# Head-pair loads in one DMA each, bucket bits carried by small DMAs, and the weight split on GpSimd, in a fused kernel of hashed attention and a gated Fourier convolution

## The chip, the core and the metric

The kernel runs on one core of one Trainium2 chip. A core has five engines with a program of their own each: TensorE (PE in the profile, with its weight loads as PEld), VectorE (DVE), ScalarE (ACT), GpSimd (POOL) and SyncE (SP), which here only issues DMAs. Each engine works through its own instructions in order. The metric is device microseconds of one execution; lower is better. Ratios are computed as the mean time of one kernel's fast runs over the mean time of the other's fast runs of the same rounds on the same chip, so they are not quite the ratio of the medians that are quoted beside them.

## The reference

Two stages follow each other. The first is attention in 4 batches of 8 heads with 768 tokens and head size 64, in which a query sees only the keys of its own bucket; the bucket is the sign pattern of six projections.

```python
q_bits = (np.einsum('bhsd,dk->bhsk', q, proj) > 0)         # 6 bits a token
k_bits = (np.einsum('bhsd,dk->bhsk', k, proj) > 0)
mask = q_bucket[:, :, :, None] == k_bucket[:, :, None, :]  # the six bits read as a number
scores = np.where(mask, scale * q @ k.T, -1e9)
attn = softmax(scores); out = attn @ v                     # the divisor gets + 1e-9
# ... heads side by side: x is (4, 768, 512) ...
x1, x2, x3 = split(x @ w_proj)                             # w_proj is (512, 1536)
x2_conv = irfft(rfft(x2, axis=1) * rfft(filter, axis=0))   # over the 768 tokens
y = x1 * x2_conv * x3
return y @ w_out                                           # (4, 768, 512)
```

## The kernel before

The kernel works on 16 head pairs. For each pair a preparation loads q and k, transposes them on TensorE, evacuates them to `tz`, multiplies with the projection (`zps`, the "bit matmuls"), and turns the signs into six rows of ±0.5, which are appended to q and k, so that one matmul yields score and bucket match together. Preparations run two pairs ahead. GpSimd copies `tz` to fp16 rows. Then come scores (`stp`), exponentials (`pt`, ScalarE), the product with v (`pv`), its evacuation (`S` on ScalarE, `T` on VectorE), and the divisors (`lt`, `rl`, `rdr`, `R`, by way of DMAs on SyncE). Weights and filter are loaded and split into two fp16 halves while the first pairs run.

```python
def nat_load(src, b, pr, which, eng):          # q, k: 4 DMAs each; v: 2
    shape = [P, 2, 3, 2, HD] if which == "v" else [P, 3, 2, 2, HD]
    t_ = natp.tile(shape, FP32, tag="nat", name=f"nat_{which}")
    for par in range(2):
        head = src[b, 2 * pr + par].rearrange("(c p j) d -> p c j d", c=3, p=P, j=2)
        if which == "v":
            eng.dma_start(t_[:, par], head)
        else:
            for j in range(2):
                eng.dma_start(t_[:, :, j, par, :], head[:, :, j, :])
    return t_
# ... prep_gen: the transposes, each half evacuated to tz on VectorE, rows copied on GpSimd ...
        with tc.high_priority(offset=200):     # the bit matmuls of both halves, at once
            for hf in range(2):
                cs = slice(HALF * hf, HALF * hf + HALF)
                zps = psW.tile([P, HALF], FP32, tag="w", name="zps")
                zs.append(zps)
                for i in (1, 0):
                    mm = nc.tensor.matmul(zps[64 * i : 64 * i + 38, :], projpad, tzs[i][:, cs])
                    # ...
        for hf in range(2):                    # eight evacuations of 6 rows
            for i, which in enumerate(("q", "k")):
                for par, r0 in ((0, 64), (1, 0)):
                    z0 = 64 * i + 32 * par
                    nc.vector.tensor_scalar(row[(which, par)][r0 : r0 + 6, cs],
                        zs[hf][z0 : z0 + 6, :], 0.0, 0.5, ALU.is_gt, ALU.subtract)
        yield 1700
# ... setup_gen, for each of four 128x1536 chunks of w_proj:
            nc.vector.tensor_copy(th, w32)
            (nc.vector if c % 2 else nc.gpsimd).tensor_tensor(tl, w32, th, ALU.subtract)
```

A generator's `yield n` ends a turn of n nanoseconds of TensorE's time; a loop deals such turns out to attention, preparation and the second stage, and so fixes the order of TensorE's program. PSUM tiles with tag "w" share four banks: `tps`, `zps`, `pv` and all of the second stage's.

The softmax here doesn't subtract the row's maximum and nothing guards it: scores larger than these inputs give would overflow.

## Time and profile before

The kernel before took 524.32 us (median of 3 runs, 521.95 to 526.36). The first lines of its profile page give the span and each engine's busy time, its share of the span, and its instructions.

```profile
span 521.2 us, 7013 instructions
## 1 busy us (share of the span) xinstructions
PE 469.4 (90%) x2552; PEld 248.6 (48%) x2552; DVE 322.5 (62%) x591; ACT 229.8 (44%) x321; POOL 156.1 (30%) x206
```

TensorE is busy nine tenths of the time. Where it is not shows the view by stretches: for each stretch of time, its length, then each engine's busy us and number of instructions, TensorE's granted clock, DMA share and rate.

```profile
core 0: us, PE busy (x) PEld busy (x) DVE busy (x) ACT busy (x) POOL busy (x), PEclk, DMA share, GB/s
...
58.00:92.00 34.00, 23.04 (x98) 10.51 (x98) 28.31 (x38) 9.93 (x14) 23.98 (x21) 0.80 0.42 114
...
120.00:270.00 150.00, 140.05 (x771) 75.48 (x770) 89.58 (x173) 72.36 (x100) 44.30 (x59) 0.98 0.26 65
270.00:425.00 155.00, 147.17 (x838) 80.44 (x836) 98.22 (x189) 78.75 (x111) 37.97 (x47) 1.00 0.19 51
...
```

Between 58 and 92 us TensorE worked 23 of 34 us at a clock of 0.80. Between 120 and 425 us it missed 18 of 305 us. The number of matmuls in parentheses will be the measure of progress below: every kernel here has 2552 of them, so whoever has issued more by a given time is ahead. The measure is rough by a few: a matmul across the border of two stretches is counted in both (counted by their starts, the leads below differ by up to 4), and matmuls are not all of one length.

A wait of ScalarE of 13.3 us and two of TensorE's waits on `tz` are in the view of waits (the engine and line that waited, whom for, us in total, times, the longest).

```profile
ACT S L275 <- DVE T L276: 13.3, 1, 13.3
...
PE zps L215 <- DVE tz L202: 5.6, 4, 2.5
...
PE tps_k L198 <- DVE tz L202: 2.2, 1, 2.2
```

VectorE was what ScalarE waited 13.3 us for. The timeline (start, duration, engine, line, operation, tiles) shows why it was late: two equal casts, and a subtraction of GpSimd.

```profile
52.13 0.41 DVE L435 CAST woh_622<-o_616 128x512 f16<-128x512 f32 x1
...
53.33 3.31 DVE L435 CAST woh_626<-o_616 128x512 f16<-128x512 f32 x1
...
56.32 3.93 POOL L438 TENSOR_TENSOR wol_620<-o_616,woh_618 128x512 f16<-128x512 f32 x1
```

The same cast took 0.41 and 3.31 us, the second of them (to 56.64 us) ending 0.3 us after the subtraction that GpSimd had begun before it (52.00 to 56.36 us); GpSimd's subtraction took 3.93 us where a later one took 1.15. The Trainium skill, "SBUF — State Buffer", "Who interferes with whom", describes VectorE's second port pair as shared with GpSimd under an exclusive lock; the trace agrees, by these durations.

### The profile page before, as it was taken

What the parts mean: (1) busy time and instruction counts of PE and PEld (TensorE: products, weight loads), DVE (VectorE), ACT (ScalarE), POOL (GpSimd) and SP (SyncE); (2) the same over time, 40 slices, a digit from 0 to 9 for tenths busy, and PEclk for the clock granted to TensorE, in tenths of its full rate; (3) what the DMA queues carried; (4) which work ended last, traced back from release to release, by engine and by line L of the source; (5) the groups of instructions that cost most, each with busy time, mean ns of one, the idle gap of its engine ahead of it and who ended that gap; (6) DMA issues with size and microseconds to landing.
All of it is one profiled execution on the core that took longest, in us unless ns stands there. A gap on an engine that the chain in (4) does not pass through costs nothing.

```text
span 521.2 us, 7013 instructions
## 1 busy us (share of the span) xinstructions
PE 469.4 (90%) x2552; PEld 248.6 (48%) x2552; DVE 322.5 (62%) x591; ACT 229.8 (44%) x321; POOL 156.1 (30%) x206
## 2 busy tenths in 40 slices
PE   4797657988998989999898998989999999999997
PEld 2343323544464545645354554645455556445553
DVE  4888987893756887353747878463645783036830
ACT  0496604883454553446365355336577310201102
POOL 4574993562414222232324131232311110000000
PEclk9898869998998999999999999999999999999999
DMA  9798514541313031324113040313010100300003
GB/s 215 186 287 218 171 32 102 123 121 34 91 32 91 1 93 32 93 91 139 45 32 91 14 109 1 93 44 120 20 32 1 33 30 1 121 1 1 0 2 121
DMA packets 82084, 39.93 MB, mean 77 GB/s; under 512 B 61953, under 2 KB 74753, under 8 KB 82049
## 3 DMA queue, kind: packets, MB, share of 16 engines
q1 hardware_dynamic: 78544, 38.62, 27.8%
q10 hardware_dynamic: 3504, 0.86, 0.8%
q8 instruction: 20, 0.33, 0.3%
q14 instruction: 16, 0.12, 0.1%
HBM read 32.97 MB, written 6.39 MB: 76 GB/s over the span
## 4 chain that ended last, share of the span: by engine, by line
PE 50%; DMA 17%; DVE 16%; issue 7%; POOL 5%; SPq 3%; ACT 2%; DVEq 0%; ACTq 0%; POOLq 0%
PE wout L488 8%; DMA R<-rdr 7%; PE pv L270 5%; DMA rdr<-rl 5%; PE stp L354 4%; PE x2b L488 3%; PE x2c L488 3%; PE zps L215 3%; PE x2a L488 2%; PE idrq L488 2%; DMA nat_v<-in_v_dram 2%; SPq L177 2%; PE fdft L488 2%; DVE U L304 1%; DMA flt_572<-in_moe_filter_fft_dram 1%
## 5 line engine op out<-in xcount | busy, mean ns | idle before, releaser
L276 DVE SCALAR_TENSOR_TENSOR T<-S,cst_sb,pv 64x512 f32<-64x512 f32 x64 | 38.9, 608 | 58.0 <-ACT S L275 57.3
L310 POOL TENSOR_TENSOR xl<-U,xh 128x768 f16<-128x768 f32 x16 | 26.5, 1654 | 97.0 <-DVE xh L308 97.0
L275 ACT COPY S<-pv 64x512 f32<-64x512 f32 x64 | 30.5, 477 | 46.1 <-PE pv L270 30.4
L215 PE MATMUL zps<-tz,projpad 128*38 128x384 f32 x128 | 29.0, 561 | 8.1 <-DVE tz L202 5.6
L198 PE MATMUL tps_q<-cst_sb,nat_q 128*128 128x128 f32 x96 | 24.9, 297 | 11.1 <-DVE T L276 6.6
L632 ACT ACTIVATE osb<-wout 128x512 f32<-128x512 f32 x24 | 14.3, 595 | 45.0 <-PE wout L488 44.9
L198 PE MATMUL tps_k<-cst_sb,nat_k 128*128 128x128 f32 x96 | 24.7, 288 | 7.7 <-DMA nat_k<-in_k_dram 2.5
L304 DVE SCALAR_TENSOR_TENSOR U<-T,vsd,R 128x768 f32<-128x768 f32 x16 | 16.5, 1032 | 23.5 <-DMA R<-rdr 20.5
L202 DVE TENSOR_SCALAR tz<-tps_q 128x384 f32<-128x384 f32 x32 | 17.6, 554 | 18.9 <-PE tps_q L198 18.4
L488 PEld LDWEIGHTS <-xh 128*128 128x128 f16 x192 | 18.9, 99 | 19.8 <-DVE xh L308 1.6
L198 PEld LDWEIGHTS tps_q<-cst_sb,nat_q 128*128 128x128 f32 x96 | 13.8, 151 | 20.4 <-DVE T L276 7.4
L359 ACT ACTIVATE pt_115<-stp,nmatch 128x768 f16<-128x768 f32 x16 | 14.5, 904 | 16.8 <-PE stp L354 16.6
L359 ACT ACTIVATE pt_111<-stp,nmatch 128x768 f16<-128x768 f32 x16 | 14.4, 901 | 15.5 <-PE stp L354 15.5
L198 PEld LDWEIGHTS tps_k<-cst_sb,nat_k 128*128 128x128 f32 x96 | 13.4, 147 | 16.4 <-issue 4.3
L359 ACT ACTIVATE pt_112<-stp,nmatch 128x768 f16<-128x768 f32 x16 | 14.4, 903 | 15.4 <-PE stp L354 15.2
L202 DVE TENSOR_SCALAR tz<-tps_k 128x384 f32<-128x384 f32 x32 | 17.5, 549 | 6.0 <-PE tps_k L198 4.0
L359 ACT ACTIVATE pt_106<-stp,nmatch 128x768 f16<-128x768 f32 x16 | 14.4, 902 | 14.9 <-PE stp L354 14.9
L359 ACT ACTIVATE pt_104<-stp,nmatch 128x768 f16<-128x768 f32 x16 | 14.4, 901 | 14.2 <-PE stp L354 7.3
L359 ACT ACTIVATE pt_110<-stp,nmatch 128x768 f16<-128x768 f32 x16 | 14.4, 902 | 11.8 <-PE pv L270 6.3
L354 PE MATMUL stp<-pr_q_0_87,pr_k_0_90 128*128 128x512 f16 x72 | 17.9, 325 | 1.6 <-ACT pt_108 L359 1.4
L354 PE MATMUL stp<-pr_q_0_86,pr_k_0_89 70*128 70x512 f16 x72 | 17.6, 333 | 1.7 <-ACT pt_104 L359 0.7
L488 PEld LDWEIGHTS <-wph_594 128*128 128x128 f16 x128 | 12.3, 98 | 13.8 <-issue 4.8
(1290 smaller groups left out, 1382.8 us busy)
## 6 DMA issues: line engine op xcount, KB each, us to landing
nat_q<-in_q_dram SPq DMA_DIRECT2D x64, 96.0 KB, 2.9
nat_v<-in_v_dram SPq DMA_DIRECT2D x32, 192.0 KB, 3.8
R<-rdr SPq DMA_DIRECT2D x32, 192.0 KB, 3.6
out_dram<-osb SPq DMA_DIRECT2D x24, 256.0 KB, 2.0
nat_k<-in_k_dram SPq DMA_DIRECT2D x56, 96.0 KB, 2.6
o_616<-in_moe_w_out_dram SPq DMA_DIRECT2D x1, 1024.0 KB, 7.5
nat_k<-in_k_dram ACTq DMA_DIRECT2D x8, 96.0 KB, 4.1
flt_572<-in_moe_filter_fft_dram SPq DMA_DIRECT2D x1, 768.0 KB, 7.1
```

Source lines behind the costliest of these rows:

```text
L198: nc.tensor.transpose(tps[:, ts(i, P)], nat[:, c3, j].rearrange("p h d -> p (h d)"), ident)
L202: nc.vector.tensor_scalar(tz[:, cs], tps, scl, None, ALU.mult)
L215: mm = nc.tensor.matmul(zps[64 * i : 64 * i + 38, :], projpad, tzs[i][:, cs])
L270: nc.tensor.matmul(pv, vpr[:, jt, :], pl[jt][:, lo_c:hi_c], start=(jt == 0), stop=(jt == NCH - 1),)
L275: nc.scalar.copy(S[rows, lo_c:hi_c], pv[HD:P, :])
L276: nc.vector.scalar_tensor_tensor(T[rows, lo_c:hi_c], in0=S[rows, lo_c:hi_c], scalar=mask[rows, :], op0=ALU.mult, in1=pv[0:HD, :], op1=ALU.add,
L304: nc.vector.scalar_tensor_tensor(U, in0=T[:, 0:SEQ], scalar=vsd, op0=ALU.add, in1=R, op1=ALU.mult)
L310: nc.gpsimd.tensor_tensor(tl, U, th, ALU.subtract)
L354: nc.tensor.matmul(stp[:, lo_c:hi_c], kp[kr, ts(jt, P)], qp[kr, lo_c:hi_c])
L359: nc.scalar.activation(pt[:, 0:SEQ], stp, AF.Exp, bias=nmatch, scale=LSCALE)
L488: nc.tensor.matmul(dest, lh, rh, start=(i == 0), stop=(i == len(terms) - 1))
L632: nc.scalar.mul(osb, po, 1.0 / YSCALE)
```

## The change

It was described as: q, k and v of a head pair in one DMA each, bucket bits by two evacuations and 6-row DMAs, weight split on POOL; divisors broadcast by one DMA per head. The last item is the same in both kernels: the diff does not touch it. The token order inside a pair changes so that a row of a load is 512 bytes (two tokens) instead of 256; the second stage's indices follow. The core of the diff, with cuts marked:

```diff
-        # nat_load: 4, 4 and 2 DMAs a pair (see above)
+        t_ = natp.tile([P, NCH, P], FP32, tag="nat", name=f"nat_{which}")
+        eng.dma_start(
+            t_,
+            src[b, 2 * pr : 2 * pr + 2].rearrange("h (c p j) d -> p (h c) (j d)", c=3, p=P, j=2),
+        )
 ...                        # prep_gen: tz in four tiles of 384 columns, 8 row copies of half size
+        for _ in range(4):
+            yield 160
         last = None
-        with tc.high_priority(offset=200):
-            for hf in range(2):        # both zps tiles, then eight evacuations
+        bt = tzp.tile([P, 2, HALF], FP16, tag="bt", name="bt")
+        for par in range(2):
+            zps = psW.tile([P, HALF], FP32, tag="w", name="zps")
+            for i, which in ((1, "k"), (0, "q")):
+                mm = nc.tensor.matmul(zps[HD * i : HD * i + HD, :], projpad, tz[(which, par)])
 ...
+            nc.vector.tensor_scalar(bt[:, par], zps, 0.0, 0.5, ALU.is_gt, ALU.subtract)
+            r0 = (64, 0)[par]
+            for i, which in enumerate(("q", "k")):
+                for j in range(2):
+                    z0 = HD * i + 6 * j
+                    nc.sync.dma_start(
+                        row[(which, par)][r0 : r0 + 6, HALF * j : HALF * j + HALF],
+                        bt[z0 : z0 + 6, par],
+                    )
-        yield 1700
+        yield 700
 ...                        # weights
-            nc.vector.tensor_copy(th, w32)
+            nc.gpsimd.tensor_copy(th, w32)
-            (nc.vector if c % 2 else nc.gpsimd).tensor_tensor(tl, w32, th, ALU.subtract)
+            nc.gpsimd.tensor_tensor(tl, w32, th, ALU.subtract)
-            nc.vector.tensor_copy(th2, o32[:, c, :])
+            nc.gpsimd.tensor_copy(th2, o32[:, c, :])
 ...                        # start: first v on ScalarE's queue, projection on GpSimd's, 11 pt buffers for 12
```

More of the change, by code (lines that the diff above doesn't have):

```diff
@@ L134 @@
     cst_sb = cp.tile([P, P + 4], FP32, name="cst_sb")
-    nc.scalar.dma_start(cst_sb, cst_d.ap())
+    nc.scalar.dma_start(cst_sb[:, 0:P], cst_d.ap()[:, 0:P])
     ident = cst_sb[:, 0:P]
     mask = cst_sb[:, P : P + 1]
-    projpad = cp.tile([P, 38], FP32, name="projpad")
+    projpad = cp.tile([P, HD], FP32, name="projpad")
     nc.vector.memset(projpad, 0.0)
-    nc.scalar.dma_start(projpad[0:HD, 0:6], proj)
-    nc.scalar.dma_start(projpad[HD:P, 32:38], proj)
+    nc.gpsimd.dma_start(projpad[0:HD, 0:6], proj)
+    nc.gpsimd.dma_start(projpad[HD:P, 6:12], proj)
+    nc.gpsimd.dma_start(cst_sb[:, P : P + 4], cst_d.ap()[:, P : P + 4])
     nmatch = cp.tile([P, 1], FP32, name="nmatch")
@@ L155 @@
         prs.append(row)
-    NPT = 12
+    NPT = 11
     pts = [cp.tile([P, SEQ + 4], FP16, name=f"pt_{i}") for i in range(NPT)]
@@ L167, in nat_load @@
     def nat_load(src, b, pr, which, eng):
-        shape = [P, 2, 3, 2, HD] if which == "v" else [P, 3, 2, 2, HD]
-        t_ = natp.tile(shape, FP32, tag="nat", name=f"nat_{which}")
-        for par in range(2):
-            head = src[b, 2 * pr + par].rearrange("(c p j) d -> p c j d", c=3, p=P, j=2)
-            if which == "v":
-                eng.dma_start(t_[:, par], head)
-            else:
-                for j in range(2):
-                    eng.dma_start(t_[:, :, j, par, :], head[:, :, j, :])
+        t_ = natp.tile([P, NCH, P], FP32, tag="nat", name=f"nat_{which}")
[3 more added lines that the diff above has]
+        )
         return t_
@@ L189, in prep_gen @@
         row = prs[g % NPR]
-        tzs = []
+        tz = {}
         for (which, scl), nat in zip((("q", QSCL), ("k", KSCL)), nats):
-            tz = tzp.tile([P, SEQ], FP32, tag=f"tz_{which}", name="tz")
-            for hf in range(2):
-                cs = slice(HALF * hf, HALF * hf + HALF)
+            for par in range(2):
                 tps = psW.tile([P, HALF], FP32, tag="w", name=f"tps_{which}")
-                for i in range(3):
-                    c3, j = divmod(3 * hf + i, 2)
-                    nc.tensor.transpose(
-                        tps[:, ts(i, P)], nat[:, c3, j].rearrange("p h d -> p (h d)"), ident
-                    )
-                    if i == 2:
-                        nc.vector.tensor_scalar(tz[:, cs], tps, scl, None, ALU.mult)
-                    yield 165
-            nc.gpsimd.tensor_copy(row[(which, 0)][0:HD, :], tz[0:HD, :])
-            nc.gpsimd.tensor_copy(row[(which, 1)][HD:P, :], tz[HD:P, :])
-            tzs.append(tz)
@@ L207, in prep_gen @@
-        last = None
-        zs = []
-        with tc.high_priority(offset=200):
-            for hf in range(2):
-                cs = slice(HALF * hf, HALF * hf + HALF)
-                zps = psW.tile([P, HALF], FP32, tag="w", name="zps")
-                zs.append(zps)
-                for i in (1, 0):
-                    mm = nc.tensor.matmul(
-                        zps[64 * i : 64 * i + 38, :], projpad, tzs[i][:, cs]
-                    )
-                    if last is not None:
-                        tc.add_manual_dep(
-                            mm.ins, last.ins.name,
-                            mybir.DependencyInfo(
-                                mybir.DependencyClass.NoSync, mybir.DependencyReason.DATA
-                            ),
-                            reason="column tiles side by side",
-                        )
-                    last = mm
@@ L227, in prep_gen @@
-        for hf in range(2):
-            cs = slice(HALF * hf, HALF * hf + HALF)
-            for i, which in enumerate(("q", "k")):
-                for par, r0 in ((0, 64), (1, 0)):
-                    z0 = 64 * i + 32 * par
-                    nc.vector.tensor_scalar(
-                        row[(which, par)][r0 : r0 + 6, cs], zs[hf][z0 : z0 + 6, :],
-                        0.0, 0.5, ALU.is_gt, ALU.subtract,
-                    )
-        yield 1700
-    def v_prep(g):
+                t_ = tzp.tile([P, HALF], FP32, tag=f"tz_{which}{par}", name="tz")
@@ new lines, in prep_gen @@
+                for c in range(3):
+                    nc.tensor.transpose(tps[:, ts(c, P)], nat[:, 3 * par + c, :], ident)
+                    if c == 2:
+                        nc.vector.tensor_scalar(t_, tps, scl, None, ALU.mult)
+                    yield 165
+                rows = slice(HD * par, HD * par + HD)
+                for j in range(2):
+                    nc.gpsimd.tensor_copy(
+                        row[(which, par)][rows, HALF * j : HALF * j + HALF],
+                        t_[HD * j : HD * j + HD, :],
+                    )
@@ new lines, in prep_gen @@
+                tz[(which, par)] = t_
+        for _ in range(4):
+            yield 160
+        last = None
+        bt = tzp.tile([P, 2, HALF], FP16, tag="bt", name="bt")
+        for par in range(2):
+            zps = psW.tile([P, HALF], FP32, tag="w", name="zps")
+            for i, which in ((1, "k"), (0, "q")):
+                mm = nc.tensor.matmul(zps[HD * i : HD * i + HD, :], projpad, tz[(which, par)])
+                if last is not None:
+                    tc.add_manual_dep(
+                        mm.ins, last.ins.name,
+                        mybir.DependencyInfo(
+                            mybir.DependencyClass.NoSync, mybir.DependencyReason.DATA
+                        ),
+                        reason="column tiles side by side",
+                    )
+                last = mm
+            nc.vector.tensor_scalar(bt[:, par], zps, 0.0, 0.5, ALU.is_gt, ALU.subtract)
+            r0 = (64, 0)[par]
+            for i, which in enumerate(("q", "k")):
+                for j in range(2):
+                    z0 = HD * i + 6 * j
+                    nc.sync.dma_start(
+                        row[(which, par)][r0 : r0 + 6, HALF * j : HALF * j + HALF],
+                        bt[z0 : z0 + 6, par],
+                    )
@@ L239, in v_prep @@
+        yield 700
+    def v_prep(g, eng=None):
         b, pr = divmod(g, NPAIR)
-        nat = nat_load(v, b, pr, "v", nc.sync)
+        nat = nat_load(v, b, pr, "v", eng or nc.sync)
         for par in range(2):
-            src = nat[:, par].rearrange("p c j d -> p (c j) d")
-            vpr = vts[g % 2][par]
-            nc.gpsimd.tensor_copy(vpr[:, :, 0:HD], src)
+            src = nat[:, 3 * par : 3 * par + 3, :].rearrange("p c (j d) -> p j c d", j=2)
+            vpr = vts[g % 2][par].rearrange("p (j c) d -> p j c d", j=2)
+            nc.gpsimd.tensor_copy(vpr[:, :, :, 0:HD], src)
@@ L245, in v_prep @@
             nc.gpsimd.tensor_tensor(
-                vpr[:, :, 64:96], src[:, :, 0:32], vpr[:, :, 0:32], ALU.subtract
+                vpr[:, :, :, 64:96], src[:, :, :, 0:32], vpr[:, :, :, 0:32], ALU.subtract
             )
             nc.gpsimd.tensor_tensor(
-                vpr[:, :, 97:P], src[:, :, 33:HD], vpr[:, :, 33:HD], ALU.subtract
+                vpr[:, :, :, 97:P], src[:, :, :, 33:HD], vpr[:, :, :, 33:HD], ALU.subtract
             )
@@ L332, in attn_gen @@
     def attn_gen():
-        nats = prep_loads(0, (nc.sync, nc.scalar))
-        prep0 = Feed(prep_gen(0, nats))
-        v_prep(0)
+        prep0 = Feed(prep_gen(0, prep_loads(0, (nc.sync, nc.sync))))
+        v_prep(0, nc.scalar)
+        late = prep_loads(1, (nc.sync, nc.sync))
         prep0.drain()
-        preps = [Feed(prep_gen(1, prep_loads(1, (nc.sync, nc.scalar))))]
+        preps = [Feed(prep_gen(1, late))]
         pv = Feed(iter(()))
@@ L514, in proj_gen @@
             ps = bank(DM, "x2a")
-            yield from group(ps, x2_terms(2 + j))
+            yield from group(ps, x2_terms(3 * j + 1))
             x1s = fbp.tile([P, DM], FP32, tag="xs", name="x1s")
@@ L519, in proj_gen @@
             ps = bank(DM, "x2b")
-            yield from group(ps, x2_terms(4 + j))
+            yield from group(ps, x2_terms(3 * j + 2))
             e_ = fbp.tile([P, DM], FP32, tag="e_", name="e_", bufs=1)
@@ L526, in proj_gen @@
             ps = bank(DM, "x2c")
-            yield from group(ps, x2_terms(j))
+            yield from group(ps, x2_terms(3 * j))
             s_, p_ = fold(ps, e_, j, fbp, 1)
@@ L588, in inv_gen @@
             cv = fbp.tile([P, SEQ], FP32, tag="cv", name="cv")
-            nc.vector.tensor_tensor(cv[:, 0:T3], asb, prq[:, 0:T3], ALU.add)
+            cvv = cv.rearrange("p (j c t) -> p c j t", j=2, c=3)
+            r_ = prq[:, 0:T3].rearrange("p (j t) -> p j t", j=2)
+            q_ = prq[:, T3 : 2 * T3].rearrange("p (j t) -> p j t", j=2)
+            a_ = asb.rearrange("p (j t) -> p j t", j=2)
+            nc.vector.tensor_tensor(cvv[:, 0], a_, r_, ALU.add)
             w_ = fbp.tile([P, T3], FP32, tag="w_", name="w_", bufs=1)
@@ L593, in inv_gen @@
             )
-            nc.vector.tensor_tensor(
-                cv[:, T3 : 2 * T3], w_, prq[:, T3 : 2 * T3], ALU.subtract
-            )
-            nc.vector.tensor_tensor(cv[:, 2 * T3 : SEQ], w_, prq[:, T3 : 2 * T3], ALU.add)
+            wv = w_.rearrange("p (j t) -> p j t", j=2)
+            nc.vector.tensor_tensor(cvv[:, 1], wv, q_, ALU.subtract)
+            nc.vector.tensor_tensor(cvv[:, 2], wv, q_, ALU.add)
             cvs[ct] = cv
@@ L632, in out_gen @@
             nc.scalar.mul(osb, po, 1.0 / YSCALE)
-            nc.sync.dma_start(ob[c // 2, c % 2], osb)
+            nc.sync.dma_start(ob[c % 3, c // 3], osb)
             yield 216
```

## The prediction

> **What bounds it now.** The busy table has PE at 469 of 521 us (90%), DVE 62%, ACT 44%, POOL 30%. By stretches (windows view), PE idles in three places. 0–17 us: start-up; first exponential at 17.75 us. 17–120 us: busy 82 of 103 us, clock 0.80 in 58–92 us. 120–425 us: 18 of 305 us idle. After that PE runs on (92 of 96 us). So TensorE is the floor; at most 45 us can be won.
>
> The largest hole is 60–73 us. ScalarE waits 13.3 us for DVE's T evacuation (longest of the waits). The chain of waits runs through DVE from 56.6 to 72.4 us: weight splits, and instructions blown up by POOL. One 128x512 cast takes 3.31 us where its twins take 0.41; a one-row copy takes 3.30; POOL's 128x512 subtraction takes 3.93 where another took 1.15. The Trainium skill, "SBUF — State Buffer", "Who interferes with whom", calls the shared VectorE/GpSimd port pair an exclusive lock; the trace agrees.
>
> **What the change does.**
> 1. Bits: 8 DVE evacuations of 6x384 (0.55 each, 4.4 us a pair) become two of 128x384 (the tz eviction of that size: 0.55). DVE loses 3.3 us a pair, 53 us in all. Instead come 8 small DMAs a pair; similar ones (lt) land in 2.1 us, issue 0.4–0.5 us.
> 2. Loads: 10 DMAs a pair become 3, in 512-byte runs where q and k had 256. SP's DMAs a pair: 15 to 16, a draw.
> 3. Weights: DVE loses about 15 us of casts and subtractions (contended), POOL gains an estimated 16 us (cast 128x1536 about 1.7, from 0.50 at 384; subtraction 3.3), less what contention took. Row copies, 4x0.82 becoming 8 of half size, add about 0.7 us a pair. POOL goes from 156 to 175–185 us, and is 85–90% busy in 30–90 us: the new risk.
> 4. TensorE's work and the broadcast of divisors are unchanged in the diff.
>
> **On the critical path.**
> - Start-up: k landed at 8–9 us; now near 6 us; evacuation plus small DMAs take about 4 us; first exponential near 14 us: −3 to −4.
> - The 60–73 us hole mostly closes: −13, but POOL's block of splits delays row copies, v copies and xl: +4.
> - 75–120 us, DVE 82% busy and setting the pace: −4 (ScalarE, 11.5 us a pair, then sets it).
> - 120–425 us: PE waits for DVE shrink: −5. Bits sit on SP's queue before the divisor DMAs; there is slack, prepared two pairs ahead: 0 to +2.
> - The tail: 0.
>
> Sum about −21: **503 us**, range 490 to 515. Chance of over 2% faster 0.82, within 2% 0.14, slower 0.04.
>
> **What would show it.** DVE busy 245–260 us; POOL 175–185 us; PE 460–468 us; first exponential at 12.5–15 us; no wait of ScalarE for T over 4 us in 50–80 us; exponentials at 0.8–1.0 us pitch there; first x2a matmul at 100–110 us instead of 119.7; packets under 512 B far fewer than 61953; bits landing in 2–4 us.
>
> **What would make it wrong.** POOL issues the splits as one block of some 27 us and starves the row copies, so that PE waits for POOL in 50–100 us: 512 or more. Bits' DMAs waiting behind bulk loads (DMA share 0.9 before 40 us), or blocking SP's queue in order so that divisors come late and the first projection starts no earlier. Or time won early returns as waits later. More is won if the clock (0.66 in 60–80 us) holds.

## More of the kernel before

One more line, of SyncE's queue, will be needed: when the first filter load was issued.

```profile
27.24 0.49 SPq L413 DMA_DIRECT2D flt_572<-in_moe_filter_fft_dram  x1
```

## The result, and the profile after

The kernel after took 501.07 us (median of 4 runs, 499.76 to 511.85, of which the longest was slow) against 523.13 us for the kernel before (4 runs); the ratio of the fast runs is 0.956, with a 95% interval of 0.950 to 0.962. Executions over 1.5% slower than the fastest of the same kernel are left out of the means. The predicted 503 us and its range hold. The lines that answer to those of before, first the page, then the stretches:

```profile
span 498.0 us, 7166 instructions
...
PE 466.5 (94%) x2552; PEld 251.0 (50%) x2552; DVE 258.9 (52%) x485; ACT 230.5 (46%) x321; POOL 183.1 (37%) x282
```

```profile
58.00:92.00 34.00, 27.56 (x121) 13.25 (x119) 15.66 (x26) 16.88 (x22) 32.56 (x32) 0.75 0.55 172
...
120.00:270.00 150.00, 146.14 (x831) 80.19 (x830) 82.39 (x154) 79.33 (x109) 51.91 (x83) 1.00 0.26 74
270.00:425.00 155.00, 154.06 (x885) 85.98 (x883) 85.23 (x168) 71.28 (x103) 36.59 (x51) 1.00 0.15 46
...
```

VectorE lost 64 us of work and GpSimd gained 27. But see where the time was won. Adding up the matmuls of the stretches, the kernel before had issued 448 by 120 us and 2057 by 425 us; the kernel after 477 and 2193. It was 29 matmuls ahead at 120 us and 136 ahead at 425 us. The 136 are worth 23.2 us (521.2 less 498.0, since little changes after 425 us), 0.17 us each, so 5 us of the gain had been won by 120 us and 18 us came between 120 and 425 us. The prediction had it the other way round: 16 to 17 us by 120 us, and 5 after it.

Why so little came early shows when the stretch from 58 to 92 us is cut in two, first for the kernel before, then for the kernel after:

```profile
58.00:75.00 17.00, 9.20 (x30) 4.05 (x30) 16.82 (x19) 2.83 (x4) 16.84 (x12) 0.67 0.45 134
75.00:92.00 17.00, 13.84 (x70) 6.46 (x69) 11.50 (x20) 7.10 (x10) 7.13 (x11) 0.93 0.40 93
```

```profile
58.00:75.00 17.00, 14.93 (x82) 7.51 (x80) 8.02 (x16) 8.85 (x12) 15.91 (x14) 0.99 0.67 226
75.00:92.00 17.00, 12.63 (x41) 5.73 (x40) 7.64 (x11) 8.03 (x11) 16.65 (x19) 0.51 0.43 117
```

The hole did close: by 75 us the kernel after was some 60 matmuls ahead, about 10 us. By 92 us half of that was gone. From 74.5 us on TensorE spent 17.1 us at half clock and issued 41 matmuls for 70; its 12.6 busy us at 0.51 would be some 6 us at full clock, an estimate from these two figures. GpSimd was busy all the time (32.6 of the 34 us), but TensorE's own wait for it there was 2.7 us. Why the clock fell there is not shown. The waits and SyncE's queue after:

```profile
ACT S L269 <- PE pv L264: 19.2, 11, 8.4
...
PE zps L211 <- DVE tz L195: 3.2, 2, 2.0
...
PE pv L264 <- POOL vt_0_131 L242: 2.7, 1, 2.7
```

```profile
21.55 1.42 SPq L226 DMA_DIRECT2D pr_q_1_93<-bt  x2
23.02 1.36 SPq L226 DMA_DIRECT2D pr_k_1_96<-bt  x2
...
28.90 0.54 SPq L407 DMA_DIRECT2D flt_574<-in_moe_filter_fft_dram  x1
```

ScalarE's wait of 13.3 us for T is gone from the list; its longest with S is now one of 8.4 us for TensorE. TensorE waits 3.2 us with the bit matmuls for `tz` where it had waited 5.6, and a wait of 2.7 us for GpSimd's copy of v is new. The small DMAs of the bits (two of them in 1.42 us) take about 0.7 us each to issue, though each carries 4.5 KB: more than most loads of 384 KB, 0.4 to 0.5 us.

### The profile page after: what moved, and what is told of

Read it like the earlier page. It is cut to its first block, busy times and chain, and to the rows that moved or that the text cites. A ratio compares the mean times of both kernels' runs of the same rounds, so it can differ in the third digit from the quotient of the medians.

```text
span 498.0 us, 7166 instructions
## 1 busy us (share of the span) xinstructions
PE 466.5 (94%) x2552; PEld 251.0 (50%) x2552; DVE 258.9 (52%) x485; ACT 230.5 (46%) x321; POOL 183.1 (37%) x282
## 2 busy tenths in 40 slices
DMA packets 57187, 40.51 MB, mean 81 GB/s; under 512 B 11712, under 2 KB 49856, under 8 KB 57152
## 4 chain that ended last, share of the span: by engine, by line
PE 75%; DMA 7%; DVE 6%; ACT 4%; POOL 3%; issue 3%; SPq 1%; DVEq 0%; ACTq 0%; POOLq 0%
PE pv L264 9%; PE stp L348 9%; PE wout L482 8%; PE zps L211 4%; PE x2a L482 4%; PE x2c L482 4%; PE x2b L482 3%; PE fdft L482 3%; DMA R<-rdr 3%; PE idrq L482 2%; PE tps_k L193 2%; DMA rdr<-rl 2%; DMA nat_k<-in_k_dram 1%; PE tps_q L193 1%; DVE U L298 1%
## 5 line engine op out<-in xcount | busy, mean ns | idle before, releaser
L193 PE MATMUL tps_q<-cst_sb,nat_q 128*128 128x128 f32 x96 | 26.5, 304 | 8.9 <-DMA nat_q<-in_q_dram 5.1
L211 PE MATMUL zps<-tz,projpad 128*64 128x384 f32 x128 | 28.2, 549 | 3.2 <-DVE tz L195 3.2
L195 DVE TENSOR_SCALAR tz<-tps_q 128x384 f32<-128x384 f32 x32 | 17.7, 554 | 22.0 <-PE tps_q L193 21.4
L353 ACT ACTIVATE pt_105<-stp,nmatch 128x768 f16<-128x768 f32 x18 | 16.2, 901 | 24.0 <-PE stp L348 23.9
L221 DVE TENSOR_SCALAR bt<-zps 128x384 f16<-128x384 f32 x32 | 17.6, 553 | 17.5 <-PE zps L211 16.7
L298 DVE SCALAR_TENSOR_TENSOR U<-T,vsd,R 128x768 f32<-128x768 f32 x16 | 18.5, 1156 | 10.8 <-DMA R<-rdr 10.6
L193 PEld LDWEIGHTS tps_q<-cst_sb,nat_q 128*128 128x128 f32 x96 | 14.4, 156 | 18.7 <-issue 6.5
L353 ACT ACTIVATE pt_107<-stp,nmatch 128x768 f16<-128x768 f32 x18 | 16.2, 900 | 11.9 <-PE stp L348 11.0
L353 ACT ACTIVATE pt_106<-stp,nmatch 128x768 f16<-128x768 f32 x18 | 16.2, 899 | 11.5 <-PE stp L348 11.4
L348 PE MATMUL stp<-pr_q_0_88,pr_k_0_91 128*128 128x512 f16 x72 | 19.6, 355 | 1.9 <-ACT pt_114 L353 0.8
L353 ACT ACTIVATE pt_108<-stp,nmatch 128x768 f16<-128x768 f32 x18 | 16.2, 901 | 11.0 <-PE stp L348 10.8
L353 ACT ACTIVATE pt_112<-stp,nmatch 128x768 f16<-128x768 f32 x17 | 15.3, 899 | 12.4 <-PE stp L348 12.2
L353 ACT ACTIVATE pt_114<-stp,nmatch 128x768 f16<-128x768 f32 x17 | 15.3, 900 | 11.9 <-PE stp L348 11.7
L348 PE MATMUL stp<-pr_q_0_87,pr_k_0_90 70*128 70x512 f16 x72 | 18.6, 349 | 1.6 <-DMA pr_k_0_90<-bt 1.0
L238 POOL CAST vt_1_132<-nat_v 128x384 f16<-128x384 f32 x8 | 4.7, 583 | 41.2 <-PE pv L264 41.2
```

The costliest lines, as they stand in the source:

```text
L193: nc.tensor.transpose(tps[:, ts(c, P)], nat[:, 3 * par + c, :], ident)
L195: nc.vector.tensor_scalar(t_, tps, scl, None, ALU.mult)
L211: mm = nc.tensor.matmul(zps[HD * i : HD * i + HD, :], projpad, tz[(which, par)])
L221: nc.vector.tensor_scalar(bt[:, par], zps, 0.0, 0.5, ALU.is_gt, ALU.subtract)
L298: nc.vector.scalar_tensor_tensor(U, in0=T[:, 0:SEQ], scalar=vsd, op0=ALU.add, in1=R, op1=ALU.mult)
L348: nc.tensor.matmul(stp[:, lo_c:hi_c], kp[kr, ts(jt, P)], qp[kr, lo_c:hi_c])
```

## The experiments

All gave correct results. All are timed against the kernel before, each in three rounds; an interval that spans the 2% mark (0.98) settles that a kernel is faster, not that it is so by 2% (weight split alone, order alone, loads cut again without the bits, turns between chunks). Theory A was mine: the gain is VectorE's 3.3 us a pair of relief. Rivals were the loads (B) and the weight split (C). The first four runs each do or undo one named part.

### Bits alone

The kernel before, with two evacuations and eight DMAs in place of the eight evacuations (the projection padded to 64 columns, 11 exponential buffers), nothing else:

```diff
-                    nc.vector.tensor_scalar(row[(which, par)][r0 : r0 + 6, cs], zs[hf][z0 : z0 + 6, :], ...)
+            nc.vector.tensor_scalar(bt[:, hf], zs[hf], 0.0, 0.5, ALU.is_gt, ALU.subtract)
+                    nc.sync.dma_start(row[(which, par)][r0 : r0 + 6, cs], bt[z0 : z0 + 6, hf])
```

> The kernel before with only the bits changed: two 128x384 evacuations and eight 6-row DMAs a pair in place of eight 6x384 evacuations; loads, weight split and row copies as before (11 exponential buffers, as the change has). Theory A (the change wins by taking 3.3 us a pair off VectorE, mostly between 120 and 425 us): DVE busy near 270 us, time 505 to 511 us, PE idle between 120 and 425 us under 8 us instead of 18; the 60 to 73 us hole stays. Rival B (the larger loads, with fewer packets and fewer DMAs, win the time): 519 us or more. Rival C (the weight split on POOL wins it, as my prediction's largest term had it): 515 us or more.

It took 527.87 us, ratio 1.007 (1.001 to 1.012). VectorE's busy time fell by 54 us, as it should, and nothing was won: theory A in this form (the relief wins by itself) falls, though the run also loads SyncE's queue, as seen next. The run was 40 matmuls behind the kernel before at 120 us (408 to 448) and level at 425 us (2054 to 2057), so it gained later what it had lost early. SyncE's queue shows the early loss:

```profile
26.10 1.42 SPq L234 DMA_DIRECT2D pr_q<-bt  x2
32.01 1.97 SPq L177 DMA_DIRECT2D nat_k<-in_k_dram  x4
...
56.21 0.96 SPq L412 DMA_DIRECT2D flt<-in_moe_filter_fft_dram  x2
```

Eight bit DMAs at about 0.7 us and ten loads at about 0.5 us a pair stand in one queue, and the filter loads, which stood behind them, were issued at 56.2 us instead of 27.2. From this came theory D: SyncE's issue time is a resource, the bits spend it, and the merged loads pay for them.

### The whole change without the bits

```diff
-            nc.vector.tensor_scalar(bt[:, par], zps, 0.0, 0.5, ALU.is_gt, ALU.subtract)
-                    nc.sync.dma_start(row[(which, par)][r0 : r0 + 6, ...], bt[z0 : z0 + 6, par])
+                    nc.vector.tensor_scalar(row[(which, par)][r0 : r0 + 6, ...], zps[z0 : z0 + 6, :], ...)
```

> The kernel after with the bits evacuated again by eight 6x384 instructions on VectorE, everything else of the change kept. Theory A: most of the gain is gone, 514 to 521 us, DVE busy near 310 us, PE idle between 120 and 425 us back to 12 us or more. Rivals B and C: at most 507 us.

It took 512.08 us, ratio 0.975 (0.971 to 0.980): worse than the change by 11 us, and outside what either side expected. Half the gain stayed without the bits.

### The weight split alone, and the change without it

> The kernel before with only the weight casts and subtractions moved from VectorE to POOL. Theory A: the hole at 60 to 73 us closes (no wait of ScalarE for T over 4 us), but POOL is then over 85% busy between 58 and 92 us and the time is given back by 92 us: 519 to 524 us. Rival C: 508 to 514 us.

The kernel before with the weight lines of the diff took 516.20 us, ratio 0.984 (0.979 to 0.988): between the two expectations.

> The kernel after with the weight casts on VectorE and the subtractions split between VectorE and POOL, as before. Theory A: little lost, 499 to 504 us; a wait of ScalarE for T comes back near 60 to 75 us, and POOL falls below 80% busy between 58 and 92 us. Rival C: 510 us or more.

The kernel after with those lines put back took 505.81 us, ratio 0.963 (0.959 to 0.968): close above theory A's range, far below rival C's. So the weight split is worth 8 us by itself and 5 us in the change (about 1%), and is not the core of it.

### Loads and all that is unnamed

The kernel after with both the bits and the weights undone:

> The kernel after with both other parts undone: bits by eight evacuations on VectorE, weights split as before; so the merged loads, the new token order and the earlier loads at the start alone. Theory A (VectorE's time) has fallen with the bits alone at 1.007 of before. Theory D: the bits' DMAs take SyncE's queue 0.70 us each (two in 1.42 us), 5.6 us a pair, and in the bits-only run the filter loads were issued at 56.2 us instead of 27.2 us; the merged loads give back about 3.5 us a pair of that queue, so that the parts pay only together. D expects the loads alone to win little: 514 to 521 us. Rival B (the loads win by themselves): 508 us or less.

It took 506.26 us, ratio 0.964 (0.958 to 0.971), with VectorE as busy as in the kernel before (322.4 us). That is 19 of the 22 us, against theory D's expectation for it, and it seemed to prove rival B. It did not: this kernel also holds everything that the change does without naming it. Two more runs took it apart.

### The loads cut again, without the bits

The loads-only kernel, with q, k and v again in 4, 4 and 2 DMAs of the sizes of before:

```diff
+        for h in range(2):
+            head = src[b, 2 * pr + h].rearrange("(c p j) d -> p c (j d)", c=3, p=P, j=2)
+            for j in range(1 if which == "v" else 2):
+                cs = slice(0, P) if which == "v" else slice(HD * j, HD * j + HD)
+                eng.dma_start(t_[:, 3 * h : 3 * h + 3, cs], head[:, :, cs])
```

> The loads-only kernel (506 us) with its loads cut again as before; so what stays of the change is the token order, the finer tz tiles, the pacing and the earlier loads at the start. If the merging of the loads is what won the 19 us there: 517 us or more. If the order and pacing won it: 505 to 511 us.

It took 507.98 us, ratio 0.973 (0.964 to 0.981). The merging of the loads was worth 1.7 us in medians there (4 to 5 us by the ratios, as the two were timed in different rounds), and the intervals overlap. Rival B, which had it win the 19 us, falls too.

### The order of the bit matmuls alone

The kernel before with the four extra turns, the bit matmuls half by half without raised priority, and the shorter closing turn; no load, evacuation, copy or DMA is changed:

```diff
-        with tc.high_priority(offset=200):
-            for hf in range(2):        # both zps, then all eight evacuations
+        for _ in range(4):
+            yield 160
+        for hf in range(2):            # one zps and its four evacuations, then the other
-        yield 1700
+        yield 700
```

> The kernel before with one thing of the change that its description does not name: the bit matmuls (zps) issued half by half after four extra turns instead of together at raised priority, and the shorter closing turn (700 for 1700). Theory F (this order of TensorE's work is part of what the loads-only run won, since in the kernel before TensorE loses some 6 us between 120 and 425 us waiting with the bit matmuls for tz): 512 to 519 us, the waits of zps for tz down from 5.6 us to under 3. If the order is worth nothing: 521 us or more.

It took 507.46 us, ratio 0.971 (0.962 to 0.980) with the same number of instructions (7013) and the kernel before at 525.20 in those rounds: better than theory F had hoped. Below are the busy line of its page, its stretches, and a line of its waits.

```profile
PE 463.0 (92%) x2552; PEld 246.9 (49%) x2552; DVE 317.7 (63%) x591; ACT 229.8 (45%) x321; POOL 157.8 (31%) x206
```

```profile
120.00:270.00 150.00, 141.95 (x806) 77.57 (x805) 97.11 (x182) 75.88 (x105) 48.40 (x63) 1.00 0.29 72
270.00:425.00 155.00, 151.83 (x877) 84.83 (x875) 98.90 (x193) 73.16 (x105) 32.55 (x39) 1.00 0.16 42
...
```

```profile
PE zps L214 <- DVE tz L202: 1.2, 1, 1.2
```

It was 19 matmuls ahead of the kernel before at 120 us and 93 at 425 us: like the change, it wins between 120 and 425 us. VectorE is as busy as before (317.7 for 322.5 us). The wait with the bit matmuls for `tz` fell from 5.6 to 1.2 us; part of it came back with other matmuls, so that TensorE's listed waits for `tz` fell only from 10.3 to 7.8 us, and all its listed waits from 46.8 to 38.3. Between 120 and 425 us its idle time fell from 17.8 to 11.2 us, and the clock there rose to full: in the trace's clock records the kernel before spends two periods of 3.4 us at half clock in that time and this one none (in the whole run 27 us before and 14 here, without the last period at the very end). Idle time (6.6 us) and clock (3.4 us) together are about 10 of the 12.6 us that the 74 matmuls are worth at 0.17 us each. The rest is not in waits too short for the list, as all gaps are in these idle times; the 0.17 us is a mean over kinds of matmul that take 0.11 to 0.22 us at full clock, and the two kernels issue different kinds in that stretch.

The granted clock is a rival that the record lets one bound. In the two profiled runs, 27 us at half clock against 14 are some 7 of the 15.6 us between them. But in the timed runs of these rounds the order alone took 505.85 us at a clock of 0.975, and the fastest run of the kernel before took 517.52 us at 0.982: some 12 us remain at a clock that is no higher. Whether the order also raises the clock is not shown. The loads-only kernels, which have this order too and add the new token order, the finer `tz` tiles and the earlier start, took 506.26 and 507.98 us: what they add is worth nothing that the runs resolve.

The order differs as follows. The compiled programs of TensorE, for the second pair's preparation, near 20 us (x2 and x4 are matmuls in a row; a trace shows two records for each bit matmul):

```
before                                             order alone
Matmult stp<-pr_q_0_86,pr_k_0_89 128x256           Matmult stp<-pr_q_0_86,pr_k_0_89 128x256
Matmult pv<-pt_104,vt_0_128 128x512                Matmult pv<-pt_104,vt_0_128 128x512
Matmult zps<-tz,projpad 38x384 x4                  Matmult zps<-tz,projpad 38x384 x2
... (4 stp, 2 pv)                                  ... (4 stp, 2 pv)
                                                   Matmult zps<-tz,projpad 38x384 x2
```

For this pair the four bit matmuls come in one run in the kernel before and in halves with the new order. By the code a run holds two of the four shared PSUM banks until eight evacuations of 0.55 us have passed, and TensorE works in order, so when `tz` is not yet evacuated or no bank is free, everything behind waits. But this picture of halves and banks does not hold where the time is won. Between 120 and 425 us the traces show the bit matmuls of all nine pairs in one unbroken run with the new order, and of seven of nine in the kernel before; and TensorE's waits for the evacuations of the bits, by which held banks would show, are 0.2 us there in the kernel before and none with the new order. What differs there is the distance: between a pair's last transpose and its first bit matmul stand 11 to 23 other matmuls with the new order, and 1 to 17 in the kernel before, 5 or fewer for five of the pairs. The waits at the bit matmuls themselves fell from 5.6 to 2.0 us in that stretch, over half of the 6.6 us of idle time. So it is shown that the order alone wins the time, and that the bit matmuls stand later and wait less; the four extra turns are the likely cause of the distance, but no run here separates priority, halving, extra turns and closing turn.

### The whole change with the loads cut again

The edit of the loads above, on the kernel after:

> The kernel after with the loads of q, k and v cut again into the pieces of before (4, 4 and 2 DMAs of 96 to 192 KB, 256-byte runs for q and k), nothing else changed. Theory D (SyncE's queue cannot carry the bits' DMAs and the cut loads at once): 512 us or more, filter loads issued after 40 us instead of 28.9. If the merging matters little: 499 to 505 us.

It took 519.75 us, ratio 0.995 (0.985 to 1.006): with the bits' DMAs present, the cut loads cost 18.7 us, where without them they cost 1.7 (by the ratios about 20 us and 4 to 5). First a line of SyncE's queue, then three of the waits:

```profile
56.83 1.38 SPq L408 DMA_DIRECT2D flt<-in_moe_filter_fft_dram  x2
```

```profile
PE hps L444 <- DVE fs L382: 15.3, 2, 13.8
...
DVE fs L382 <- POOL fe L410: 13.4, 2, 11.9
...
POOL fe L410 <- DMA flt<-in_moe_filter_fft_dram: 8.9, 1, 8.9
```

The filter loads were issued at 56.8 us; the sums on GpSimd (`fe`) waited 8.9 us for them, VectorE's `fs` 13.4 us for those, and TensorE's filter transform (`hps`) 15.3 us for that, 13.8 of it at once. Between 12 and 58 us SyncE issued 41 DMAs in the kernel before, filling 20.2 of the 46 us (durations of the queue's records, added); 49 filling 31.8 in the kernel after; 71 filling 40.2 with the bits alone, and 72 filling 41.3 here. Theory D holds: by these sums the queue was nearly full in the two kernels that won nothing, and in both the filter loads came about 29 us later than in the kernel before.

### VectorE's load put back

The kernel after with six evacuations a pair added that nobody reads:

> The kernel after with six useless 6x384 evacuations a pair added on VectorE (into a scratch tile nobody reads): VectorE's load of before without the DMAs taken away. If VectorE's time is what the bits win once the queue can carry them, 508 to 514 us, like the run without the bits (512). If the win of the bits lay elsewhere (order of instructions, copies), at most 504 us.

It took 506.27 us, ratio 0.965 (0.958 to 0.973), between the two expectations and therefore undecided: 46 us more VectorE work than the kernel after cost 5 us, half of what taking the bits out cost. If VectorE's time has a worth here it is about a tenth of its size, but 5 us is 1%, the intervals overlap, and differences of this size are not assigned to a cause below.

### Setup loads on another queue

The bits-only kernel with tables, filter and weights loaded from GpSimd's queue:

> The bits-only kernel with the loads of tables, filter and weights issued from POOL's queue instead of SyncE's. Theory D (the bits' DMAs hold up these loads in SyncE's queue, which costs the bits-only run 7 us by 120 us): filter loads issued before 35 us, lead over the kernel before no longer negative at 120 us, 512 to 519 us. Rival E (the landing time of the bits' own DMAs, or the order, costs it): 522 us or more.

It took 528.48 us, ratio 1.006. This reads like theory E, but the run did not isolate what it was built for. The table loads now started at once and shared the DMA engines with the second pair's q and k, whose issues went on until 16.4 us; the first exponential came at 22.8 us where the bits-only kernel had 18.2. The filter loads were indeed early (33.0 us), but at 120 us the run was still 30 matmuls behind; that an early win was lost again at the start is my reading, not shown. The cut loads above are the cleaner test.

### Two attempts to do better

Since GpSimd was busy 32.6 of 34 us between 58 and 92 us, the eight casts of the weights were moved on to ScalarE:

```diff
-            nc.gpsimd.tensor_copy(th, w32)
+            nc.scalar.copy(th, w32)
-            nc.gpsimd.tensor_copy(th2, o32[:, c, :])
+            nc.scalar.copy(th2, o32[:, c, :])
```

> The kernel after with the eight weight casts moved on from POOL to ScalarE (half idle between 58 and 92 us), the subtractions left on POOL. POOL is busy 32.6 of 34 us there. If POOL's queue is what gives back the hole that the change closed, POOL loses about 8 us of work there and the run takes 494 to 498 us; if not, 500 us or more.

It took 507.25 us, ratio 0.965 (0.959 to 0.972): slower than the change by 6 us. GpSimd's busy time in that stretch fell to 28.4 us and TensorE issued 129 matmuls there for 121, but by 120 us the run was 4 matmuls behind the kernel after, and by 425 us 20 behind, in a part of the program where no line was changed.

The other attempt only dealt turns out between the weight chunks (a `yield 1250` after each of eight):

> The kernel after with a turn of the setup's work ended after each weight chunk, so that the attention's instructions are placed between the chunks instead of behind the block; no instruction added. POOL is over 95% busy between 58 and 92 us in the kernel after and the lead won by 75 us (9.5 us) is down to 3 us at 92 us. If the order of POOL's block is what gives it back: 493 to 498 us. If POOL's amount of work is: 499 us or more.

It took 506.90 us, ratio 0.970 (0.962 to 0.979), also slower than the change; GpSimd was still busy 33.1 us in that stretch. Neither the amount nor the order of GpSimd's work there, changed one at a time, brought the time back; in both runs a period at half clock came at the same place again (13.7 us from 77.1 us on with the casts on ScalarE, 10.2 us from 80.1 us on with the turns). The kernel after stays the fastest of all that were run.

### All runs side by side

Medians and ratios to the kernel before of the same rounds; the last columns are the matmuls issued by 120 and by 425 us, less the kernel before's 448 and 2057 (from the stretches of each profile).

| kernel | median us | ratio | by 120 us | by 425 us |
|---|---|---|---|---|
| the change | 501.07 | 0.956 | +29 | +136 |
| without the weight split | 505.81 | 0.963 | +19 | +111 |
| without bits and weight split | 506.26 | 0.964 | +24 | +96 |
| with useless evacuations | 506.27 | 0.965 | +22 | +79 |
| weight casts on ScalarE | 507.25 | 0.965 | +25 | +116 |
| turns between weight chunks | 506.90 | 0.970 | +7 | +102 |
| order of bit matmuls alone, on before | 507.46 | 0.971 | +19 | +93 |
| without bits and weight split, loads cut | 507.98 | 0.973 | +17 | +89 |
| without the bits | 512.08 | 0.975 | +6 | +72 |
| weight split alone, on before | 516.20 | 0.984 | +13 | +45 |
| with the loads cut | 519.75 | 0.995 | -49 | +22 |
| bits alone, on before | 527.87 | 1.007 | -40 | -3 |
| bits alone, setup loads from GpSimd's queue | 528.48 | 1.006 | -30 | -25 |

## Why the prediction was right or wrong, point by point

The total was right, 503 against 501; the sum behind it was not. Its terms were wrong in both directions and cancelled, so the hit is in good part luck.

- **"TensorE's work … unchanged in the diff."** This is the step that failed. The work is unchanged, its order is not, and the order alone takes the kernel before from 525 to 507 us (15.7 us in means of the fast runs, 17.7 in medians). I had read the `high_priority` block and the changed turns in the diff and costed them at nothing.
- **"120–425 us: PE waits for DVE shrink: −5."** It was −18 (107 matmuls at 0.17 us). I had taken TensorE's idle time in the view by stretches as a ceiling: it fell there from 17.8 to 4.8 us, a difference of 13, while the progress is worth 18. The Trainium skill, "Trainium Kernel Development and Optimization", "Performance Expectations", warns that matmul busy time is a bad metric for closeness to the limit because matmuls are pipelined; this case does not test that, since most of the 5 us has another source: the kernel before spent 6.8 us there at half clock, which is 3.4 us, and the kernel after none. The rest lies in the rough 0.17 us.
- **"75–120 us … −4", and the hole "mostly closes: −13, … +4", and start-up "−3 to −4".** By 120 us all of it together was worth 5 us, not 16 to 17. The hole itself did close, and some 10 us were won by 75 us; the term for what comes back was too small (+4): TensorE ran at half clock from 74.5 to 91.6 us. GpSimd was 85% busy between 30 and 90 us (50.9 of 60 us), as I had expected for that stretch, and 96% between 58 and 92 us. The first exponential came at 15.59 us (predicted near 14, 12.5 to 15), 2.2 us earlier than before.
- **"SP's DMAs a pair: 15 to 16, a draw."** The count was right and the time wrong: 0.66 us and more to issue a bit DMA, not 0.4–0.5, and 31.8 us of queue for 20.2 in the stretch from 12 to 58 us. It was a draw only because the loads were merged; without that it costs 18.7 us. I had costed the merging of the loads as a gain by itself, and by itself it is worth less than the runs resolve.
- **"DVE loses 3.3 us a pair, 53 us in all."** The work did go (busy 258.9 us, within 245–260), but the gain per us is small or none: 54 us taken away in the bits-only run won nothing overall (with SyncE's queue against it), and 46 us put back cost 5, which is not clear of the noise between kernels.
- **Marks.** POOL 183.1 us (175–185), PE 466.5 us (460–468), packets under 512 B 11712 for 61953, and no wait of ScalarE for T: right. Exponentials at a pitch of 0.8–1.0 us: wrong, ScalarE was busy 16.9 of 34 us between 58 and 92. First x2a matmul at 100–110 us "instead of 119.7": I had misread the trace; the first one before starts at 113.7 us, 119.7 is the first with a listed wait. After, it starts at 110.1. The landing times of the bits' DMAs are not in the profile; the scores waited 1.0 us for them, once.

What stays open: which part of the new order does it (priority, halving, turns); what the order is worth inside the change, as no run takes it out there; how much of the gain is the granted clock, and what sets it; and why bits and weight split, which on top of the rest win 0.5 us and lose 6 us alone, win 5 us together. Kernels whose edits lie before 120 us lost a further 16 and 12 matmuls between 120 and 425 us (casts on ScalarE, and turns, against the change), so the order that the scheduler happens to find is worth several us here, and differences of about 1% between these variants are not assigned to a cause.

## What to carry to other kernels

Before costing the named parts of a change, compare the order of the bottleneck engine's program: moving a few matmuls to a later place was worth 16 to 18 us here by itself, while taking 53 us of work off another engine was worth anything from −4 to 11 us, by what stood around it (bits alone, and the change without the bits). Count the issue time of DMAs on a queue, not their number or bytes, and look at what stands behind them in the queue; two parts that each gain nothing alone may need each other. Locate a gain in time, by counting the bottleneck engine's instructions at fixed moments, before believing the sum that forecast it.

## What the Trainium skill lacked or had wrong

- "DMA: Bandwidth & Descriptors", "Issuing engines are not separate DMA queues": it says that the time on the sequencer to initiate a DMA "is usually small relative to the DMA itself". For a load of 384 KB issued in 0.4 to 0.5 us that fits. For a 6-row DMA of 4.5 KB the issue took 0.66 us and more, longer than for most of the large loads, and 72 issues filled 41.3 of 46 us, so that the queue was nearly full. How long these small DMAs themselves took is not in the profile. The page gives no issue time for this chip by shape.
- "SBUF — State Buffer", "Who interferes with whom": agrees (0.41 and 3.31 us for the same cast). It does not say this: closing such a conflict by giving GpSimd all the work left GpSimd busy 32.6 of 34 us there, and the whole change had won only 5 us by 120 us.
- No page that was consulted names the order of an in-order engine's program as a thing to compare first; here it won 16 to 18 us by itself, where the whole change won 22.
